# Six of seven convolution taps moved from VectorE to ScalarE and an adding DMA

## The chip, the cores and the metric

The kernel runs on one core of one Trainium2 chip. The core has five engines with a program each: TensorE (PE in the profile), VectorE (DVE), ScalarE (ACT), GpSimd (POOL) and SyncE (SP, which only issues DMAs here). Sixteen DMA engines carry all transfers. The metric is the device time of one launch in microseconds; lower is better.

## The reference

Two blocks follow one another. First a causal depthwise convolution with 7 taps over the sequence; the weights are soft-maxed over the taps and shared by the 24 channels of a head. Then a dense layer with silu and a second dense layer.

```python
w = np.exp(weight - weight.max(-1, keepdims=True)); w = w / (w.sum(-1, keepdims=True) + 1e-09)  # (8, 7)
x_pad = np.concatenate([zeros(B, 6, D), x], axis=1)      # x: (8, 4096, 192)
out = np.einsum('hk,bskhg->bshg', w, windows(x_pad))     # 7 taps, 8 heads of 24 channels
h = out.reshape(32768, 192) @ moe_w_in                   # (192, 2048)
return (h * (1 / (1 + np.exp(-h)))) @ moe_w_out          # (2048, 192)
```

(The lines are shortened; `windows` stands for the gather of seven shifted rows.) Everything is float32.

## The kernel before

The 32768 tokens are worked off in 32 blocks of 1024 (NB). A block holds two halves of 512 tokens: channels lie on partitions, 64 channels of the first half on partitions 0 to 63 and the same 64 of the second half on 64 to 127; the 192 channels make three channel groups k = 0, 1, 2. So one tile of 128x512 is one channel group of a block.

A block goes through these stages:

- *Load and turn* (`load`, L181; `turn_in`, L465). SP loads the block's tokens into the tile `nat` (two of them, used in turn). VectorE turns each channel group into `xt`, of which there is one only; its six first columns are the halo, filled by `halo_in` with a small copy on Pool (L486) or a memset (L480) and a DMA.
- *Convolution* (`conv`, L490 to L502). For channel group k and tap i the source is `xt` shifted by i columns, the target the same channel group of `nat`, which holds the sum. Tap 0 is a ScalarE activation with the tap's weights as scale (L496) and writes `nat`; taps 1 to 6 are a VectorE scalar_tensor_tensor (L499) each, `nat = xt * tap + nat`. That is 18 of them in a block.
- *Spread and windows* (`spread`, L516; `win`, L533 and L536). SP copies `nat` into `dups`, and VectorE forms sums and differences of the channel groups of the two halves, `win`.
- *Products* (`product`, L625, and `plain`, L642). The first dense layer is done by a scheme that saves multiplications: 5 groups (g) of 15 products (r), each summed in PSUM banks in three chains. ScalarE copies intermediate banks into tiles `u` (L674), VectorE combines them with other banks (L668), ScalarE takes the silu (L686, L691) into tiles `g`.
- *Down products* (`sum_g`, L709; `out_slot`, L741). VectorE forms differences of `g` tiles (`t`), and PE multiplies by the second layer's weights. ScalarE copies parts out of the accumulators (`yx`, `cmb`; L799, L804, L807), VectorE adds them (L819), turns them back (L829), and SP stores them (L838).

The tiles `u` are ten in number and are kept in a list, `free`: a step that needs one takes the first (`free.pop(0)`), and the step that has read it last appends it. The list is handled while the program is built, in the order in which the steps are written; the waits that it makes necessary are put in from the use of the tiles.

The order of all steps is written out by hand in the string `PLAN`: one block's stretch is some 130 slots, each with tokens that `step` (L858) turns into calls. A token is a name with digits; a prefix `-` means the block before, `=` two before, `+` the next. `P` is a product, `L` a plain one, `u`, `X`, `a`, `b`, `S` the copies, sums and silus on a product chain, `D` and `t` the down products of the block before, `sp` the spread, `w` the windows. `v.ki` is `conv(b + 1, k, i)`, so the convolution belongs to the next block. The tokens `v` stand in this order: 20 and 10 at the end of the stretch before; 00, 21, 22, 11, 12, 23, 13, 01, 14, 24, 02, 03, 25, 15, 26 among the down products; 16, 04, 05, 06 among the first products. `START` is the same for the first blocks. `pin` keeps an instruction in its written place on its engine; what isn't pinned (the halo copy on Pool, for one) may be moved by the scheduler. DMAs that SP issues form a queue in order; so do those that Pool issues.

The main loop runs over b from 3; with the `v` tokens meaning block b + 1, the main loop convolves blocks 4 to 31, and `START` the earlier ones.

Of the kernel before, what the change touches and what calls it, by code (L numbers as in the profile page):

```python
# [11 lines left out]
AF = mybir.ActivationFunctionType  # L12
ALU = mybir.AluOpType
# [4 lines left out]
def kernel(  # L18
# [24 lines left out]
    nc = tc.nc  # L43
# [111 lines left out]
    def pin(ins):  # L155
        return tc.keep_in_program_order(ins)
# [61 lines left out]
    for k in range(NK):  # L218
        rows_k = hot[SQ * k : SQ * k + SQ]
        for sign, base in ((1, 0), (-1, grp - 1)):  # L220
            pool.affine_select(
                out=rows_k,
                in_=rows_k,
# [7 lines left out]
    for e in range(2):  # L231
        half = one_hot[R * e : R * e + R].rearrange("p (a c) -> p a c", a=2)
        pool.affine_select(
            out=half,
            in_=half,
# [254 lines left out]
    def conv(b, k, i):  # L490

        src = xts[b][:, k, i : i + TB]
        dst = nats[b][:, k, :, :].rearrange("p k c -> p (k c)")
        tap = taps[:, k, i : i + 1]
        if i == 0:
            pin(nc.scalar.activation(dst, src, AF.Copy, scale=tap))  # L496
        else:
            pin(
                nc.vector.scalar_tensor_tensor(  # L499
                    out=dst, in0=src, scalar=tap, in1=dst, op0=ALU.mult, op1=ALU.add  # L500
                )
            )  # L502
# [153 lines left out]
    us, free = {}, []  # L656
# [201 lines left out]
    def step(b, token):  # L858
# [19 lines left out]
        elif name[0] in "uXabS":  # L878
            sums_h(b, name, *digits)
        elif name == "t":  # L880
            sum_g(b, *digits)
        elif name[0] == "D":
            i, (j, e) = int(name[1]), digits
            for half in range(2) if i == 3 and b == NB - 1 else (None,):
                out_slot(b, j, i, e, half)
        elif name[0] in "Mzyx":
            merge(b, name, *digits)
        elif name == "o":
            turn_out(b, *digits)
        elif name == "st":  # L890
            store_out(b, *digits)
        elif name == "dp":
            next(downs)
        elif name == "cp":
            copy_plain(b, *digits)
        elif name == "go":
            pool.tensor_copy(warm, nats[1][:, digits[0], 0, 0:1])
            for g in (2, 3):
                for e in range(2):
                    combine(g, e)  # L900
        elif name == "ld":
            if b + 1 < NB:
                load(b + 1, digits)
        elif b + 1 < NB:
            {"i": turn_in, "ha": halo_in, "v": conv, "sp": spread, "w": win}[name](
                b + 1, *digits[: 1 + (name == "v")]
            )
# [122 lines left out]
    for j in (1, 2):  # L1030
        load_in(j, nc.sync)
    turn_in(0, 2)
    conv(0, 2, 0)
    for n in range(2):
        act.copy(dups[0][:, n, 0, :], by_pe[0][n])
    for i in range(1, K):
        conv(0, 2, i)
    src = nats[0][:, 2, :, :].rearrange("p k c -> p (k c)")
# [72 lines left out]
```

## Time and profile before

| | |
|---|---|
| median of 3 runs | 2348.94 us (2348.9 to 2348.98) |
| span of the profiled execution, first to last instruction | 2347.5 us |
| median of the runs less that span | 1.4 us |
| granted TensorE clock | 1.000 |
| chain that ended last | PE 99% |
| DMA traffic | 106.56 MB, mean 45 GB/s |
| Pool's software queue (q0) | 448 packets, 1.58 MB |

The page of a profile shows one execution. The profiled execution has no time of its own in the list of runs; its span and the difference above stand for it. For each engine the page gives the busy time, its share of the span and the number of instructions. A row of a group has line, engine and operation, what is written and read, then the count, the busy time and the mean of one in ns, then the idle time of that engine just before these instructions and what ended most of it. A timeline row has start and length in us, then the operation, and in brackets the idle time before it with what ended it. A DMA row has the issuing queue, the count, the size and the median time from issue to landing. PEld is the load of weights into TensorE, which runs beside the matmuls.

### The profile page before, as it was taken

What the parts mean: (1) busy time and instruction counts of PE and PEld (TensorE: products, weight loads), DVE (VectorE), ACT (ScalarE), POOL (GpSimd) and SP (SyncE); (2) the same over time, 40 slices, a digit from 0 to 9 for tenths busy, and PEclk for the clock granted to TensorE, in tenths of its full rate; (3) what the DMA queues carried; (4) which work ended last, traced back from release to release, by engine and by line L of the source; (5) the groups of instructions that cost most, each with busy time, mean ns of one, the idle gap of its engine ahead of it and who ended that gap; (6) DMA issues with size and microseconds to landing.
All of it is one profiled execution on the core that took longest, in us unless ns stands there. A gap on an engine that the chain in (4) does not pass through costs nothing.

```text
span 2347.5 us, 43988 instructions
## 1 busy us (share of the span) xinstructions
PE 2340.3 (100%) x17630; PEld 1061.0 (45%) x17630; DVE 2099.6 (89%) x2877; ACT 1187.3 (51%) x2275; POOL 96.8 (4%) x168
## 2 busy tenths in 40 slices
PE   9999999999999999999999999999999999999998
PEld 4344444444444444434444444444444444444445
DVE  8899989899899998998998999989999989899876
ACT  4345644456544466444564445654446644456443
POOL 4920000000000000000000000000000000000000
PEclk9999999999999999999999999999999999999999
DMA  7232212222121221222221222212222212222111
GB/s 158 52 66 48 47 27 47 38 53 53 29 41 36 53 53 31 39 43 46 53 49 31 42 38 53 53 29 42 36 53 53 38 33 45 43 53 44 20 24 25
DMA packets 451245, 106.56 MB, mean 45 GB/s; under 512 B 423584, under 2 KB 428704, under 8 KB 451040
## 3 DMA queue, kind: packets, MB, share of 16 engines
q1 hardware_dynamic: 447392, 101.78, 23.7%
q8 instruction: 138, 2.26, 0.4%
q0 software_dynamic: 448, 1.58, 0.3%
q10 hardware_dynamic: 3200, 0.39, 0.1%
q14 instruction: 67, 0.55, 0.1%
HBM read 31.46 MB, written 25.17 MB: 24 GB/s over the span
## 4 chain that ended last, share of the span: by engine, by line
PE 99%; DVE 0%; ACT 0%; issue 0%; ACTq 0%
PE ps L741 47%; PE ps L625 42%; PE ps L642 5%; PE ps L762 2%; PE ps L571 2%; PE ps L1010 1%; PE ps L423 0%; DVE t L709 0%; ACT g L686 0%; DVE cmb L163 0%; ACT u L163 0%; DVE osb L163 0%; DVE osb L829 0%; DVE g L668 0%; PE ps L449 0%
## 5 line engine op out<-in xcount | busy, mean ns | idle before, releaser
L625 PE MATMUL ps<-win,wr 64*128 64x512 f32 x1550 | 720.3, 597 | 0.0
L741 PE MATMUL ps<-g,wo 128*32 128x512 f32 x2976 | 702.4, 593 | 0.0
L625 PE MATMUL ps<-win,ws 64*128 64x512 f32 x1550 | 631.3, 595 | 0.0
L741 PE MATMUL ps<-t,wo 128*32 128x512 f32 (+2 forms) x4528 | 545.7, 446 | 0.0
L674 ACT COPY u<-ps 128x512 f32<-128x512 f32 x775 | 446.8, 586 | 173.6 <-PE ps L625 161.4
L741 PE MATMUL ps<-t,wx 128*32 128x512 f32 x2976 | 495.5, 592 | 0.1
L625 PE MATMUL ps<-dup,wr 64*128 64x512 f32 x868 | 425.4, 593 | 0.0
L499 DVE SCALAR_TENSOR_TENSOR nat<-xt,taps,nat 128x512 f32<-128x512 f32 x564 | 411.3, 753 | 3.8 <-ACT nat L496 3.6
L686 ACT ACTIVATE g<-g 128x512 f32<-128x512 f32 x465 | 286.1, 633 | 231.5 <-DVE g L668 231.5
L804 ACT COPY yx<-ps 32x512 f32<-32x512 f32 x150 | 86.9, 579 | 574.0 <-PE ps L741 572.3
L709 DVE TENSOR_TENSOR t<-g 128x1024 f32<-128x1024 f32 x248 | 300.6, 1219 | 51.1 <-PE ps L741 43.4
L625 PEld LDWEIGHTS ps<-win,wr 64*128 64x128 f32 x1550 | 275.6, 186 | 150.4 <-issue 67.8
L668 DVE TENSOR_TENSOR g<-u,ps 128x512 f32<-128x512 f32 x465 | 311.2, 680 | 28.8 <-PE ps L625 14.6
L625 PE MATMUL ps<-dup,ws 64*128 64x512 f32 x682 | 324.2, 599 | 0.0
L709 DVE TENSOR_TENSOR t<-g,t 128x1024 f32<-128x1024 f32 x248 | 301.8, 1217 | 12.2 <-PE ps L741 9.4
L741 PEld LDWEIGHTS ps<-t,wo 128*32 128x32 f32 x4528 | 186.7, 110 | 274.1 <-issue 247.6
L625 PEld LDWEIGHTS ps<-win,ws 64*128 64x128 f32 x1550 | 254.7, 186 | 110.5 <-issue 40.8
L686 ACT ACTIVATE g<-ps 128x512 f32<-128x512 f32 x465 | 266.8, 597 | 41.1 <-PE ps L625 38.4
L668 DVE TENSOR_TENSOR ps<-u,ps 128x512 f32<-128x512 f32 x310 | 214.7, 692 | 43.7 <-ACT g L686 19.0
L741 PE MATMUL ps<-g,wx 128*32 128x512 f32 x1488 | 250.5, 592 | 0.0
L741 PEld LDWEIGHTS ps<-g,wo 128*32 128x32 f32 x2976 | 170.2, 110 | 120.9 <-issue 118.9
L741 PEld LDWEIGHTS ps<-t,wx 128*32 128x32 f32 x2976 | 120.5, 110 | 217.5 <-issue 202.3
(90 smaller groups left out, 1764.5 us busy)
## 6 DMA issues: line engine op xcount, KB each, us to landing
dup<-nat SPq DMA_DIRECT2D x345, 128.0 KB, 2.3
nat<-in_x_dram SPq DMA_DIRECT2D x382, 64.0 KB, 2.4
out_dram<-osb SPq DMA_DIRECT2D x376, 64.0 KB, 2.0
raw<-in_moe_w_out_dram SPq DMA_DIRECT2D x8, 384.0 KB, 3.6
raw<-in_moe_w_in_dram SPq DMA_DIRECT2D x12, 192.0 KB, 4.7
ws<-wr POOLq DMA_DIRECT2D x8, 192.0 KB, 5.0
raw<-in_moe_w_in_dram SPq DMA_DIRECT2D x6, 128.0 KB, 3.1
xt<-xt SPq DMA_DIRECT2D x31, 4.5 KB, 1.9
```

Of the source, the lines that this page charges most:

```text
L499: nc.vector.scalar_tensor_tensor(out=dst, in0=src, scalar=tap, in1=dst, op0=ALU.mult, op1=ALU.add)
L571: nc.tensor.matmul(hs[a, n, e], rows(wr[j], e)[:, a, k, :], rows(d, e)[:, n, k, :], start=k == 0, stop=k == NK - 1,)
L625: nc.tensor.matmul(to[:, cols], raw(g, *LEFT[e][r], e), rhs[:, cols], start=first, stop=True, skip_group_check=True,)
L642: nc.tensor.matmul(banks[PLAIN_BANKS[n and 1 + e]][:, cols], rows(wr[j] if own == e else ws[j], e)[:, a, k, :], rows(dups[b], e)[:, SLOT[e ...
L668: pin(nc.vector.tensor_tensor(out_, u, v, op=op))
L674: pin(nc.scalar.copy(us[b, g, o][:, cols], t1[:, cols]))
L686: pin(nc.scalar.activation(h, src, AF.Silu))
L709: pin(nc.vector.tensor_tensor(t[i // 2][:, i % 2, :], u, v, op=ALU.subtract))
L741: nc.tensor.matmul(accs[b][at][SQ * q : SQ * q + SQ, to], lhs[:, e, SQ * k : SQ * k + SQ], rhs[:, e, ts(q, TB // 4) if i == 5 else to], st ...
L762: nc.tensor.matmul(banks[DOWN_BANKS[k]][R * n : R * n + R, :], wo[j][:, a, e, R * k : R * k + R], gs[b, j, a][:, n, e, :], start=j == 0 an ...
L804: pin(nc.scalar.copy(to, acc[3 * (name[0] == "x") + k][n:P, :]))
L1010: nc.tensor.matmul(by_pe[k][n], rows(diag, n)[:, k, i, :], rows(xts[0], n)[:, k, i : i + TB], start=i == 0, stop=i == K - 1,)
```

## The change

In `conv`, taps 1 to 6 (the second to the seventh) of blocks 4 to 31 take another form. A spare tile z is taken from the front of the list `free`; ScalarE multiplies the shifted source by the tap's weights into z; a DMA on Pool's queue adds z to the channel group of `nat`; and z is appended to the list at once. Blocks 0 to 3 and tap 0 stay as they are, and `PLAN` and `START` stay unchanged, so each tap keeps its place in the written order.

```diff
         if i == 0:
             pin(nc.scalar.activation(dst, src, AF.Copy, scale=tap))
+        elif b > 3:
+            z = free.pop(0)
+            pin(nc.scalar.activation(z, src, AF.Copy, scale=tap))
+            pin(nc.gpsimd.dma_start(out=dst, in_=z, accum_op=ALU.add))
+            free.append(z)
         else:
             pin(
                 nc.vector.scalar_tensor_tensor(
```

In the built program the adding DMAs stand on Pool's queue in the order of the tokens. Each waits for its ScalarE multiply and for the adding DMA before it on the same channel group. A ScalarE instruction that writes a tile z or u waits for the adding DMA that last read that tile. The halo copy on Pool stands between the DMAs of taps 05 and 06.

## The prediction

> **What bounds the kernel now.** I read the page first, then the timeline of single blocks, then the waits. The page says which engine has no idle time:
>
> ```profile
> span 2347.5 us, 43988 instructions
> PE 2340.3 (100%) x17630; PEld 1061.0 (45%) x17630; DVE 2099.6 (89%) x2877; ACT 1187.3 (51%) x2275; POOL 96.8 (4%) x168
> L499 DVE SCALAR_TENSOR_TENSOR nat<-xt,taps,nat 128x512 f32<-128x512 f32 x564 | 411.3, 753 | 3.8 <-ACT nat L496 3.6
> ```
>
> PE bounds it; the row to be replaced (L499) is VectorE work that lies beside PE. The wait list gives the length of a block, since the halo copy on Pool runs once in each: 1368.0/19 = 72.0 us.
>
> ```profile
> POOL xt L486 <- ACT u L674: 1368.0, 19, 72.4
> PEld ps L625 <- DVE ps L668: 57.8, 214, 0.8
> PEld ps L625 <- ACT u L674: 15.6, 61, 0.6
> ```
>
> How much of the 72.0 us is PE's own work? In the timeline two matmul halves start every 0.43 us (1264.41, 1264.84, 1265.27). Each matmul of the source leaves two records. A block has 75 products, so 75 x 0.428 = 32.1 us; the plain part is 12 full-width records, 6 pairs or 2.6 us; the down part has 320 full and 64 quarter-width records, four at a time, 34.3 + 1.7 us. Together 70.7 us. So at most 1.3 us a block is stall, and no relief of another engine can give more than 28 x 1.3 = 37 us. The two lower lines say that VectorE and ScalarE both end such short waits.
>
> Then one block, in windows (PE, PEld, DVE, ACT, POOL busy; clock; DMA share; GB/s):
>
> ```profile
> 1226.00:1235.00 9.00, 9.00 (x104) 3.02 (x100) 8.54 (x10) 2.27 (x4) 0.00 (x0) 1.00 0.66 134
> 1235.00:1259.00 24.00, 24.00 (x262) 8.19 (x256) 21.01 (x27) 3.28 (x8) 0.00 (x0) 1.00 0.04 6
> 1259.00:1276.00 17.00, 17.00 (x86) 8.97 (x84) 15.54 (x25) 12.88 (x26) 0.19 (x1) 1.00 0.27 50
> 1276.00:1295.00 19.00, 19.00 (x89) 11.54 (x90) 17.05 (x27) 16.34 (x31) 0.00 (x0) 1.00 0.26 43
> ```
>
> The reader is to see that in the down stage (to 1259) ScalarE and the DMA engines are nearly free, while in the product stage (from 1259) ScalarE is 76 to 86% busy and its copies of PSUM banks (L674) set when PE may write these banks again.
>
> **The change, part by part.** 18 taps in each of 28 blocks, 504 of the 564 rows of L499.
>
> *VectorE* loses 504 x 0.729 us (411.3/564) = 367 us, 13 us a block. Fourteen of the 18 lie in the down stage, where PE seldom waits for VectorE; four (1261, 1263, 1270, 1272 us) in the product stage. Gain on the path: between 0 and 1.3 us a block; I take 0.2, since only the four count, and the waits above are each short.
>
> *ScalarE* gets 504 multiplies. The nearest row is its first tap, L496, which the next instruction follows 0.62 us later (1217.15 to 1217.77): 312 us, busy 51 to 64%. In the down stage they fill an idle stretch of 17.8 us. In the product stage the taps 16, 04, 05 and 06 stand in front of bank copies and silus, each 0.6 us; the gaps there are 0.3 to 1.0 us, so each makes the next copy 0 to 0.6 us late, and PE after it. Between 0 and 2.4 us a block; I take 0.4.
>
> *Pool* gets 504 issues of 0.65 us (the Pool issues of L347 ran 523 to 878 ns), 328 us on an engine that is idle. But Pool is in order, and each adding DMA waits for the one before it on the same channel group, as it reads and writes the same tile. What is queued behind such a wait is every later tap, and once a block the halo copy (0.19 us), which has 13 us until SP needs it (its DMA is issued at 1284). Who waits for the DMA itself: the spread DMAs (sp.1 at 1272, sp.0 and sp.2 in the next block), and, because a spare tile goes back into the free list at once, ScalarE at its reuse. That is the new wait: bank copies of the product stage now get tiles whose DMA must have read them.
>
> *The chain.* Call L the time from one adding DMA's issue to that of the next that depends on it, I = 0.65 us the issue. Taps 21 and 22 go early (about 1226 and 1226 + L). The others are released when ScalarE has done the silu at 1233.93:
>
> ```profile
> 1227.21 0.63 ACT L686 ACTIVATE g<-g 128x512 f32<-128x512 f32 x1
> 1233.93 0.63 ACT L686 ACTIVATE g<-g 128x512 f32<-128x512 f32 x1 [6.09 <-DVE g L668]
> 1252.36 0.58 ACT L804 COPY yx<-ps 32x512 f32<-32x512 f32 x1 [17.80 <-PE ps L741]
> 1267.19 0.59 ACT L674 COPY u<-ps 128x512 f32<-128x512 f32 x1 [0.63 <-PE ps L625]
> 1270.66 0.58 ACT L674 COPY u<-ps 128x512 f32<-128x512 f32 x1 [1.05 <-PE ps L625]
> ```
>
> so tap 11 issues at T = 1235.2. In Pool's order 11, 12, 23, 13, 01, 14, 24, 02, 03, 25, 15, 26, 16, 04 the issues fall at T + 0, L, L+I, 2L, 2L+I, 3L, 3L+I, 3L+2I, 4L+2I, 4L+3I, 4L+4I, 5L+3I, 5L+4I, 5L+5I. The copies that reuse these tiles: the one at 1267.19 (T + 32.0) takes tap 26's, done at 6L+3I, so L may be 5.0; the one at 1263.28 (T + 28.1) takes tap 03's, done at 5L+2I, so 5.4. Tap 05 is multiplied in its place behind the copy at 1269.1 (issue T + 35.3), tap 06 follows one L later and ends at T + 35.3 + 2L; its tile is wanted by a copy at T + 42.3 (1205.43 one block earlier). That gives L = 3.5; but this bank is next written six products after its own, 2.6 us, of which 0.9 go to the matmul's end and the copy, so PE feels it from about L = 4.2. Above 4.2 a block loses 2 us for each us of L, above 5.0 six to eight, since that many links stand ahead.
>
> *L itself* is not in the trace: there is no adding DMA. The nearest rows:
>
> ```profile
> dup<-nat SPq DMA_DIRECT2D x345, 128.0 KB, 2.3
> ws<-wr POOLq DMA_DIRECT2D x8, 192.0 KB, 5.0
> xt<-xt SPq DMA_DIRECT2D x31, 4.5 KB, 1.9
> xt<-in_x_dram POOLq DMA_DIRECT2D x2, 1.5 KB, 3.1
> xt<-in_x_dram SPq DMA_DIRECT2D x1, 1.5 KB, 2.6
> ```
>
> Low end: 128 KB more than almost nothing cost 0.4 us, so 256 KB plain 1.9 + 0.8 = 2.7. High end: the Pool row scaled to 256 KB, 1.9 + 3.1 x 4/3 = 6.0; it ran in the start-up, with the DMA engines busy, and the down stage has a share of 0.04. Value: 1.9, twice 0.8 because the target is read too, 0.5 for Pool instead of SP (3.1 against 2.6), 0.2 for waking Pool: 4.2 to 4.3, nearest to the quiet SBUF-to-SBUF row. That is at the knee.
>
> A rule on this price: the Trainium skill's page "DMA: Bandwidth & Descriptors", section "Anatomy of one DMA", has 2.0 us and bytes/436e3 for a Pool DMA, which for 256 KB would make an estimate of 2.6 us and the chain cost nothing; it does not name adding ones, and no row here shows one. Its section "Rules for kernel authors" speaks against the change: an adding DMA must wait for the completion of an earlier one on the same bytes, which is the chain above.
>
> *Sum* a block: -0.2 (VectorE) + 0.4 (ScalarE's places) + 0.3 (L at 4.3, two links of 0.1 and some spill) = +0.5 us, times 28 = +14 us. The first four blocks, start and end are not touched. Against the profiled execution's span, 2347.5 + 14 = 2361.5; the median of the runs, 2348.94, lies 1.4 us above that span, so 2363.
>
> **The rivals.**
> 1. *The chain is too slow.* With L = 5.5, 32 us after T are no longer enough: 6L+3I = 35.0 against 32.0, then taps 05 and 06 behind; about 7 us a block, 196 us, 2545. With L = 6.0, 11 us a block, 2657. For it: the Pool row of 5.0 us. Against: that row's traffic.
> 2. *Other sign: VectorE's relief pays.* If L stays under 4.2 and the product stage's stalls are mainly VectorE's (57.8 us of waits against 15.6 for ScalarE), 0.3 to 1.2 us a block come back: 8 to 34 us, 2315 to 2341. It decides when the four ScalarE insertions cost less than the four VectorE removals. Against: ScalarE's own gaps there are just as short.
> 3. *Hidden on all sides.* PE is saturated, both effects cancel within 0.2% (4.7 us, about what a measurement of this kernel can tell from no change): 2344 to 2354.
>
> **How the numbers follow.** Forecast (0.2 to 2% slower, 2354 to 2396): 0.38. Rival 1 (above 2396): 0.32. Rival 2: 0.22. Rival 3: 0.08. So faster 0.22, same 0.08, slower 0.70. The likeliest one's own range is 2354 to 2396; 8 in 10 need part of rivals 1 and 2: from 2332 (about half of rival 2) to 2580 (L of about 5.6, beyond which I leave 0.1).
>
> **What the profile after would show.** L499's row at 60, ScalarE near 1500 us, POOL near 420 us, 504 new issues "nat<-u" of 256 KB on POOLq with a landing near 4 us: right. If they land above 5 us, ScalarE's copies and multiplies wait for DMA, PE shows idle in the product stage, and the halo period grows by the same amount: rival 1. If the period falls under 72.0: rival 2. The prediction is wrong above all if L is off by half a microsecond or more, or if the tiles' reuse distance is not what the order of the free list makes it.

## The result and the profile after

The changed kernel takes 2362.43 us (median of four runs, 2360.49 to 2365.5) against 2348.92 us before: a ratio of 1.0058, 95% interval 1.0044 to 1.0072. The forecast was 2363 and slower. The profiled execution is the fastest of the four (2360.49 us); its span is 2358.8 us, 11.3 us more than before, while the medians lie 13.5 us apart. These lines of its page answer to the lines shown of before:

```profile
span 2358.8 us, 45531 instructions
PE 2350.1 (100%) x17630; PEld 1053.1 (45%) x17630; DVE 1784.5 (76%) x2373; ACT 1488.6 (63%) x2779; POOL 531.0 (23%) x672
q0 software_dynamic: 73024, 133.73, 33.7%
L500 POOL DMA_DIRECT2D nat<-u x504 | 431.9, 957 | 1598.0 <-ACT u L499 643.4
nat<-u POOLq DMA_DIRECT2D x504, 256.0 KB, 4.0
dup<-nat SPq DMA_DIRECT2D x345, 128.0 KB, 3.0
```

VectorE lost 315 us of busy time, ScalarE got 301, Pool issues 504 DMAs. They land 4.0 us after their issue (median; 3.2 to 6.2). SP's spread DMAs now land in 3.0 us instead of 2.3. That is the adding DMAs' doing: in the runs below it is 2.3 us without them and 2.6 with half their bytes. The wait list shows the wait that the prediction named, ScalarE's bank copies at reused tiles, and a longer PE wait on a silu (8.5 us in 30 waits before):

```profile
ACT u L679 <- DMA nat<-u: 28.3, 24, 2.4
PEld ps L630 <- ACT u L679: 29.0, 88, 1.3
PEld ps L630 <- ACT g L691: 27.7, 59, 0.6
```

In one block's timeline of ScalarE it is the copy that was expected at T + 42.3, which reuses tap 06's tile:

```profile
1282.01 0.58 ACT L679 COPY u<-ps 128x512 f32<-128x512 f32 x1 [0.27 <-PE ps L630]
1283.46 1.79 ACT L679 COPY u<-ps 128x512 f32<-128x512 f32 x3 [0.87 <-DMA nat<-u]
```

Where the 11.3 us lie is seen best from block to block. The copy into `cmb` runs once in each block; the distance of its starts in ScalarE's timeline is the block's length. The usual block is the median of the 28 that carry the change:

| kernel | usual block, us | 28 x (usual - 72.14) | sum above the usual block | blocks over 0.15 us above it |
|---|---|---|---|---|
| before | 72.14 | 0 | 0.1 | 0 |
| changed | 72.37 | 6.4 | 5.1 | 9 |

6.4 + 5.1 = 11.5 us is the difference of the two spans. So there are two costs: 0.23 us in every block, and a second one in nine blocks only, up to 1.46 us in one. Not all nine are the DMAs' doing: two of them, the first and the 23rd (0.35 and 0.23 us), are as uneven in the run below that leaves the taps out (0.35 and 0.33). The second cost may also be why the four runs lie 5 us apart; only one of them has a profile, so this is not shown.

### The profile page after: what moved, and what is told of

Read it like the earlier page. It is cut to its first block, busy times and chain, and to the rows that moved or that the text cites. A ratio compares the mean times of both kernels' runs of the same rounds, so it can differ in the third digit from the quotient of the medians.

```text
span 2358.8 us, 45531 instructions
## 1 busy us (share of the span) xinstructions
PE 2350.1 (100%) x17630; PEld 1053.1 (45%) x17630; DVE 1784.5 (76%) x2373; ACT 1488.6 (63%) x2779; POOL 531.0 (23%) x672
## 4 chain that ended last, share of the span: by engine, by line
PE 98%; DVE 1%; DMA 0%; ACT 0%; SPq 0%; issue 0%; ACTq 0%
PE ps L746 47%; PE ps L630 42%; PE ps L647 5%; PE ps L767 2%; PE ps L576 2%; PE ps L1015 1%; DVE t L714 0%; DMA dup<-nat 0%; PE ps L423 0%; ACT g L691 0%; DMA nat<-u 0%; SPq L843 0%; DVE g L673 0%; DVE cmb L163 0%; ACT u L163 0%
## 5 line engine op out<-in xcount | busy, mean ns | idle before, releaser
L500 POOL DMA_DIRECT2D nat<-u x504 | 431.9, 957 | 1598.0 <-ACT u L499 643.4
L630 PE MATMUL ps<-win,ws 64*128 64x512 f32 x1550 | 638.3, 599 | 0.9 <-ACT u L679 0.9
L499 ACT ACTIVATE u<-xt,taps 128x512 f32<-128x512 f32 x504 | 340.0, 717 | 1.1
L824 DVE TENSOR_TENSOR cmb<-cmb,ps 96x512 f32<-96x512 f32 x150 | 102.2, 681 | 181.7 <-ACT yx L809 180.7
```

The source lines that it names most:

```text
L499: pin(nc.scalar.activation(z, src, AF.Copy, scale=tap))
L500: pin(nc.gpsimd.dma_start(out=dst, in_=z, accum_op=ALU.add))
L630: nc.tensor.matmul(to[:, cols], raw(g, *LEFT[e][r], e), rhs[:, cols], start=first, stop=True, skip_group_check=True,)
L824: pin(nc.vector.tensor_tensor(out_, u, v, op=ALU.add))
```

## The experiments

All were timed beside the kernel before, which took 2349.04 to 2349.07 us there.

**ScalarE and VectorE without the DMAs.**

```diff
             pin(nc.scalar.activation(z, src, AF.Copy, scale=tap))
-            pin(nc.gpsimd.dma_start(out=dst, in_=z, accum_op=ALU.add))
             free.append(z)
```

> Taps two to seven of blocks 4 to 31 are multiplied on ScalarE into the spare tile, but nothing adds the tile (the sum of these taps is left out). So ScalarE's insertions and VectorE's relief stay, the adding DMAs are gone. Theory (the terms of the prediction): -0.2 us for VectorE and +0.4 us for ScalarE's places remain, +0.3 us for the DMAs' links goes: about 2355, 2351 to 2358. Rival A (ScalarE's places cost all of it, the DMA waits are hidden): 2360 to 2364, as the changed kernel. Rival B (the DMAs cost all of it, and VectorE's relief outweighs ScalarE's places): below 2347.

Measured: 2356.91 us, ratio 1.0032 (1.0021 to 1.0044); the usual block 72.39. So 5.5 us of the change's 13.5 are the DMAs' by the medians (3.3 by the spans of the profiled executions), and they are not in the usual block.

**VectorE's relief alone** (the diff stands against the changed kernel).

```diff
         elif b > 3:
-            z = free.pop(0)
-            pin(nc.scalar.activation(z, src, AF.Copy, scale=tap))
-            pin(nc.gpsimd.dma_start(out=dst, in_=z, accum_op=ALU.add))
-            free.append(z)
+            return
```

> Taps two to seven of blocks 4 to 31 are left out altogether: VectorE's relief alone, nothing on ScalarE, no DMA. Theory: 0.2 us a block come back, 2343; bounds 2312 (all of the 1.3 us a block that PE stalls) to 2349 (nothing). If VectorE ends most of PE's stalls, as the wait list's 57.8 us against 15.6 us for ScalarE could be read: 2315 to 2330.

Measured: 2348.54 us, ratio 0.9997 (0.9988 to 1.0007), a usual block of 72.09 to 72.10 us. So no gain is clear of the noise: 0.5 us by the medians, 0.05 us by the usual block, and at most 2.8 us, 0.1 a block, by the interval. Theory's 0.2 was too much, and the hope of rival 2 is gone altogether. PE's waits on VectorE did not leave with the work; the row of before had 57.8 us in 214:

```profile
PEld ps L627 <- DVE ps L670: 47.4, 160, 0.7
PEld ps L627 <- ACT u L676: 15.3, 60, 0.6
```

So most of them belong to the product chains themselves (PE, copy, combine, PE) and not to the convolution's place between them, and the 10 us of waits that did go left the time as it was.

**ScalarE's insertions alone.**

```diff
         elif b > 3:
             z = free.pop(0)
             pin(nc.scalar.activation(z, src, AF.Copy, scale=tap))
-            pin(nc.gpsimd.dma_start(out=dst, in_=z, accum_op=ALU.add))
+            pin(
+                nc.vector.scalar_tensor_tensor(
+                    out=dst, in0=src, scalar=tap, in1=dst, op0=ALU.mult, op1=ALU.add
+                )
+            )
             free.append(z)
```

> The kernel before with the ScalarE multiplies into spare tiles added, which nobody reads; the sum stays on VectorE. So ScalarE's insertions alone. Theory: +0.4 us a block, 2360 (2354 to 2368). Rival A (ScalarE's places are the whole of the change's cost and VectorE's relief adds nothing): 2362 to 2366. Rival B (ScalarE's places are free, the DMA waits are the cost): 2348 to 2351.

Measured: 2356.43 us, ratio 1.003 (1.0019 to 1.0042), a usual block of 72.39 us. The diff stands against the changed kernel. ScalarE's insertions cost 7.4 us, neither nothing nor all. With the first two runs the parts nearly add: 7.4 (ScalarE) - 0.5 (relief) + 5.5 (DMAs) = 12.4 of 13.5. What is missing is the relief itself: beside the insertions it gives nothing (2356.91 us with it, 2356.43 without), and 7.8 for both together + 5.5 = 13.3 of 13.5.

**Eleven spare tiles** (`hot` is moved in the same way as `zeros`; run twice, the profile is the second one's).

```diff
-    upool = ctx.enter_context(tc.tile_pool(name="up", bufs=10))
+    upool = ctx.enter_context(tc.tile_pool(name="up", bufs=11))
-    zeros = const.tile([P, P], F32, name="zeros") 
+    zeros = upool.tile([P, TB], F32, tag="u", name="zeros")[:, 0:P]
-    free.extend(upool.tile(...) for _ in range(10))
+    free.extend(upool.tile(...) for _ in range(11))
```

> The changed kernel with eleven spare tiles in the list instead of ten (two constants used in the start-up move into this pool to make room; the result is complete). The copy that reuses tap 06's tile is now the next one on ScalarE, 0.86 us later, and tap 05's multiply no longer waits for tap 04's DMA. Theory: the wait of ScalarE's copies for the adding DMAs, 28.3 us in all in the changed kernel, falls to below 8 us, and the time to 2354 to 2359. Rival A (ScalarE's places): 2361 to 2364, with the waits gone all the same.

Measured: 2359.66 us, ratio 1.0043 (1.0027 to 1.006), just above the theory's 2354 to 2359.

> The run with eleven tiles again, for its profile: the first one's profiled execution was disturbed and can't be read. Theory now: usual blocks stay at 72.37, the uneven ones (eight above 72.5 in the changed kernel) become fewer or smaller, ScalarE's copies wait below 8 us for adding DMAs instead of 28.3: 2359 to 2360. Rival: the uneven blocks are as many, and the gain comes from an even shorter usual block.

Measured: 2359.32 us, ratio 1.0047 (1.0032 to 1.0062). The usual block stays at 72.38; six blocks instead of nine are uneven, with 3.5 us instead of 5.1. The waits at reused tiles:

```profile
ACT u L679 <- DMA nat<-u: 6.6, 9, 1.3
DVE t L714 <- DMA dup<-nat: 10.6, 3, 3.7
```

So tile reuse carries a part of the uneven blocks, as expected: about 3 us by the medians (of the changed kernel's runs, which spread over 5), 1.5 by the sum above the usual block. The second line is another kind, below.

**The four middle taps earlier.**

```diff
-    "... -D2.30 v.02 | ... -D5.30 v.03 | -D0.10 v.25 | -D3.21 -z1.0 v.15 ... -x2.1 v.26 ..."
+    "... -D2.30 v.02 v.03 v.25 v.15 v.26 | ... -D5.30 | -D0.10 | -D3.21 -z1.0 ... -x2.1 ..."
```

> The changed kernel with the tokens of taps 03, 25, 15 and 26 moved in the written list to stand right behind tap 02, so that ScalarE multiplies them in its idle stretch ahead of the copies of the accumulators (yx, cmb) instead of between them. The result is complete. Theory now: ScalarE's places cost 7.4 us (e3), and they cost it where PE's plain products wait for the late yx copies (23.5 us of waits in e3, none before), so most of it goes: 2354 to 2357, and a usual block falls from 72.37 to 72.15 us. Rival (as the prediction had it: the four places in the product stage, taps 16, 04, 05 and 06): 2361 to 2364, a block of 72.37.

Measured: 2364.02 us, ratio 1.0061 (1.0046 to 1.0076), a usual block of 72.38. My theory of that hour fell. The 23.5 us of PE waits on `yx` did vanish, but they had cost nothing: the kernel before has the same pause of 0.84 us at this place, put down to "issue". The totals agree: before has 69.4 us of "issue" in 218 at this line of the code, the run with ScalarE's insertions 45.9 in 190 and the 23.5 in 28. (The moved multiplies also wait 104.9 us for reused tiles, so the time of this run alone would not settle it; the pause does.) Here is its row of before, then that of the run with ScalarE's insertions alone, from PE's weight-load timelines:

```profile
1258.67 0.18 PEld L642 LDWEIGHTS ps<-dup,ws 64*128 64x128 f32 x1 [0.84 <-issue]
```

```profile
1262.46 0.18 PEld L651 LDWEIGHTS ps<-dup,ws 64*128 64x128 f32 x1 [0.84 <-ACT yx L808]
1278.68 0.29 PEld L634 LDWEIGHTS ps<-dup,wr 64*128 64x128 f32 x2 [0.59 <-ACT g L695]
```

The label changed, the pause did not. The row at 1278.68 has no fellow in the kernel before; it led to the next two runs.

**Only the last four places.** ScalarE multiplies, read by nobody, in the places of taps 16, 04, 05 and 06; VectorE keeps the sum.

```diff
+            if (k, i) in ((1, 6), (0, 4), (0, 5), (0, 6)):
+                z = free.pop(0)
+                pin(nc.scalar.activation(z, src, AF.Copy, scale=tap))
+                free.append(z)
```

> The kernel before with ScalarE multiplies into spare tiles, read by nobody, only in the places of taps 16, 04, 05 and 06, in the product stage (e3 had all 18). The sum stays on VectorE and the result is complete. Theory now: these four cost nothing or little, the others' places carry e3's 7.4 us: 2348.5 to 2351. Rival (the prediction's place): 2354 to 2356.5, as e3.

Measured: 2354.65 us, ratio 1.0024 (1.0014 to 1.0033), a usual block of 72.34. The prediction's place was right after all: these four carry 0.20 of the 0.25 us a block.

**The same without tap 06** (the list of places ends at `(0, 5)`).

> As the run with the last four places, but with ScalarE multiplies only in the places of taps 16, 04 and 05; tap 06's, which stands right ahead of a run of four silus, is gone. The sum stays on VectorE and the result is complete. Theory now: in that run PE waited 0.59 us once a block for the last of those silus, so tap 06's place alone costs the 0.20 us a block: 2348.5 to 2350. Rival (each of the four a quarter): 2352.5 to 2354.

Measured: 2351.42 us, ratio 1.0011 (1.0001 to 1.002), a usual block of 72.22. Between theory and rival: tap 06's place alone costs 0.12 us a block, the other three 0.08 together. PE's waits on these silus fall from 25.1 us in 58 to 8.5 in 30, as before. In ScalarE's timeline of the run with the last four, tap 06's multiply is the row at 1274.80, right ahead of the silus; the last of them frees the bank that PE waits for:

```profile
1274.80 0.73 ACT L500 ACTIVATE u<-xt,taps 128x512 f32<-128x512 f32 x1
1275.43 0.62 ACT L696 ACTIVATE g<-g 128x512 f32<-128x512 f32 x1
1275.95 1.56 ACT L696 ACTIVATE g<-ps 128x512 f32<-128x512 f32 x3
```

```profile
1277.56 0.29 PEld L635 LDWEIGHTS ps<-dup,wr 64*128 64x128 f32 x2 [0.59 <-ACT g L696]
```

**Tap 06 behind the silus, in the changed kernel.**

```diff
-    "... P8.0 u1.4 v.06 S5.0 | ... S3.0 a0.0 S2.4 | ... S3.4 | ... b1.4 S4.4 | ..."
+    "... P8.0 u1.4 S5.0 | ... S3.0 a0.0 S2.4 | ... S3.4 | ... b1.4 S4.4 v.06 | ..."
```

> The changed kernel with tap 06's token moved in the written list to stand behind the four silus instead of ahead of them (ten tiles, result complete). Theory now: a usual block falls from 72.37 to 72.15 or 72.20 us, 5 to 6 us in all; the uneven blocks may also get rarer, since the copy that reuses this tap's tile is two copies further: 2355 to 2358. Rival (the place is not the cause): 2361 to 2364.

Measured: 2358.12 us, ratio 1.0039 (1.0025 to 1.0054). The usual block falls to 72.27, by 0.10 us, nearly tap 06's 0.12; 72.15 to 72.20 had been expected, and the time lies at the upper edge of its range. Nine blocks stay uneven, with 5.5 us.

**Half the columns.**

```diff
-            pin(nc.gpsimd.dma_start(out=dst, in_=z, accum_op=ALU.add))
+            pin(nc.gpsimd.dma_start(out=dst[:, 0 : TB // 2], in_=z[:, 0 : TB // 2], accum_op=ALU.add))
```

> The changed kernel whose adding DMAs add only the first 256 of 512 columns (the other half of the sum of taps two to seven is left out): 128 KB each, all else the same. Theory now: the DMAs' 5.5 us (2362.4 less e1's 2356.9) come from a few blocks in which they and SP's transfers hold each other up; with half the bytes the landing falls from 4.0 to about 3.4 us, the uneven blocks go, and the time is e1's: 2356.5 to 2359. Rival (a steady cost of each DMA, Pool's issue or the semaphores): 2361 to 2363, with even blocks.

Measured: 2356.94 us, ratio 1.0033 (1.002 to 1.0046): the time of the run without any DMA (2356.91). The landing is 3.0 us, and the sum above the usual block is 0.8 us, as without DMAs (0.7). So neither the 504 issues nor their semaphores cost anything here; the longer transfer of the full columns does.

**Longer links.**

```diff
             pin(nc.gpsimd.dma_start(out=dst, in_=z, accum_op=ALU.add))
+            pin(nc.gpsimd.dma_start(out=dst[:, 0:64], in_=z[:, 0:64], accum_op=ALU.add))
```

> The changed kernel with a second small adding DMA (64 columns, 32 KB) behind each of the 504, on the same bytes, so that each link of the chain is longer by one small DMA (those columns are then added twice, and the result is not the reference's). L goes from about 4.3 to 6.5 to 7 us and the issue from 0.85 to 1.7 us. Theory, by the prediction's chain (6L+3I and what follows it against the 32 us to the copy): 16 to 24 us a block, 450 to 670 us in all: 2810 to 3030. Rival (the chain has slack that the recurrence does not see, as the reuse order or PE's slack is larger): below 2600.

Measured: 3640.82 us, ratio 1.5488 (1.5463 to 1.5514), blocks of 113.7 to 122 us: 46 us a block instead of 16 to 24. My expectation missed what an in-order queue does. Pool's timeline of this run shows it (L500 the tap's DMA, L501 the small one):

```profile
1803.34 0.84 POOL L500 DMA_DIRECT2D nat<-u  x1 [1.86 <-DMA nat<-u]
1806.89 0.86 POOL L501 DMA_DIRECT2D nat<-u  x1 [2.71 <-DMA nat<-u]
1807.43 1.19 POOL L500 DMA_DIRECT2D nat<-u  x1
1811.32 0.86 POOL L501 DMA_DIRECT2D nat<-u  x1 [2.70 <-DMA nat<-u]
1811.85 1.19 POOL L500 DMA_DIRECT2D nat<-u  x1
```

The small DMA stands in the queue waiting for the large one just issued, so no other channel group's large DMA can be in flight meanwhile. A pair takes 4.1 to 4.4 us here, so 18 of them nearly 80 us, in a block that had 72. Between one block's last pair and the next block's first another 25 us pass (1843.30 to 1868.18 in the same timeline). In the changed kernel the interleaving of three channel groups hides a part of L; here it is gone. ScalarE's copies then wait 910 us in all for these DMAs. The granted TensorE clock was 0.842 in this run against 1.000 before; how much of the 46 us the lower clock adds was not separated.

**Eleven tiles and tap 06 later together.**

> Eleven tiles and tap 06's token behind the four silus, together (result complete): the best form of the change that these runs point to. Theory: the two gains add, 2362.4 - 2.8 - 5.5 = 2354, 2352 to 2357; still above the kernel before, since VectorE's relief gives nothing (0.4 us in the run of the relief alone) and tap places and traffic are left. Rival (the gains are the same one): 2357 to 2360.

Measured: 2357.13 us (2355.47 to 2357.93), ratio 1.0033 (1.002 to 1.0046). The usual block is 72.27 and ScalarE's copies wait 2.2 us in all, but six blocks stay uneven with 5.2 us. The gains add only in part: 3.1 and 4.3 us alone, 5.3 together, at the border of what theory and rival had expected. It is the fastest complete form of the change here, and still 8 us above the kernel before. The run of the relief says why none can be much better than before: leaving the taps out altogether gains 0.5 us.

**What is left of the uneven blocks.** In the chain of waits of the changed kernel's profile one such block reads like this, first the chain, then VectorE's timeline:

```profile
1375.46 1.60 SPq L843
1377.70 3.75 DMA dup<-nat
1381.47 1.24 DVE t L714
```

```profile
1376.69 1.21 DVE L714 TENSOR_TENSOR t<-g 128x1024 f32<-128x1024 f32 x1
1381.47 1.23 DVE L714 TENSOR_TENSOR t<-g 128x1024 f32<-128x1024 f32 x1 [3.57 <-DMA dup<-nat]
```

VectorE stands still for 3.57 us ahead of the sum `t`, and PE then idles 0.5 us. The sum takes a buffer in which the stores' `osb` stood, so by the code it is the three stores that it must wait for; the profile names a spread DMA, which SP issued right behind them. SP's three stores took 2.5 us to issue instead of the usual 1.41. SP's queue did that before as well, in the same block, and there the same sum waited 0.64 us, put down to a store, and the block kept its 72.14 us:

```profile
1224.49 1.41 SPq L838 DMA_DIRECT2D out_dram<-osb  x3
1368.79 2.42 SPq L838 DMA_DIRECT2D out_dram<-osb  x3
```

```profile
1372.90 1.23 DVE L709 TENSOR_TENSOR t<-g 128x1024 f32<-128x1024 f32 x1 [0.64 <-DMA out_dram<-osb]
```

So the likeliest reading is that a late store meets the first adding DMA and seven spread DMAs (DMA share 0.96 to 0.98 there), and lands later still: the slowest of the three landed after 4.1 us, before after 3.0. Which of the two kinds of DMA ends VectorE's wait was not separated by a run.

With eleven tiles such chains stand at 1157, 1375 and 1810 us, three or six blocks apart. The rhythm is older than the change: in the kernel before, from 936 to 2018 us, every third block (every 216.4 us) has three stores that take 1.9 to 2.9 us to issue. The DMA queue that the profile calls "instruction" (q8) has a packet in the same 3 to 4 us in all eight groups of three stores that took over 1.8 us there, and in two of the 47 others. So SP's delay goes along with a packet of that queue; that the packet is the cause was not tested. Four of the nine uneven blocks of the changed kernel (3.6 of the 5.1 us), and the four that remain with eleven tiles beside the first and the 23rd, are such third blocks.

## Why the prediction was right, and where its terms were not

The time (2363 against 2362.4), the sign and the chain of causes held, but all three terms of the sum were too large. In us for the 28 blocks: VectorE -5.6, measured -0.5; ScalarE's places +11.2, measured +7.4; the DMAs +8.4, measured +5.5. The errors nearly cancel, so that the time was met within 1 us is luck; the sign and the two costs are not.

- *PE bounds the kernel.* Right: 1.4 us a block is all that is not PE's own work, and the relief of another engine was bounded by it. (The prediction's 72.0 us is the halo copy's wait; with the copy's own 0.19 it is the block's 72.14.)
- *VectorE's relief, -0.2 us a block.* Mis-sized: about -0.02 by the time, -0.05 by the usual block. The step that failed is the reading of the wait list, that "only the four count, and the waits above are each short" leaves something to gain; 47.4 of the 57.8 us stay without the taps. VectorE's busy time fell by 315 us, not 367.
- *ScalarE's places, +0.4 us.* Right in kind and place, mis-sized: 0.25 us a block, of which tap 06 has 0.12, the taps 16, 04 and 05 together 0.08, and the other fourteen 0.05. ScalarE's total rose to 1489 us, against 1500 forecast.
- *The issue, 0.65 us.* 0.854 us (median), so POOL is busy 531 us instead of some 420; it did not matter, as the run with half the columns shows.
- *L, 4.2 to 4.3 us.* In the run with longer links 3.55 us from issue to dependent issue (1803.34 to 1806.89 above), with no other large adding DMA in flight; in one block of the changed kernel 4.35 between taps 05 and 06 (1275.76 to 1280.11 in Pool's timeline) and 5.86 between taps 21 and 22, beside SP's transfers. So the value lay between two cases, and the knee at 4.2 was met in some blocks only. Its part of 0.2 us for waking Pool rests on no row; in the changed kernel an issue follows the end of its multiply by 0.29 us (1230.97 to 1231.26).
- *The issue times.* For taps 03 and 04 it was not the links that set them, as the prediction's list has it: in the same timeline Pool waits for ScalarE's multiply, which stands behind other ScalarE work (4.16 us for tap 03, 0.43 for tap 04). The reuse was read rightly all the same: all 24 waits of copies for adding DMAs are at the one copy that the prediction named for tap 06's tile.
- *The DMAs' term, +0.3 us a block ("two links of 0.1 and some spill").* The sum was nearly right (8.4 against 5.5 us), its shape was not: the usual block pays nothing, although its copy waits 0.9 us, as the prediction's slack allows; seven blocks pay 0.2 to 1.5 us (the nine less the two that are uneven without DMAs). The prediction had left out that SP's transfers are themselves made later by the adding DMAs.
- *Rival 1 (chain too slow)* did not come. That PE pays many times over when the chain no longer fits was confirmed by the longer links, but its size there was set by the in-order queue, and perhaps by the lower clock, and not by the formula.
- *Rival 2 (relief pays)* is excluded by the run of the relief alone.

On the price of an adding DMA: the rule of the Trainium skill's page "DMA: Bandwidth & Descriptors", section "Anatomy of one DMA", makes an estimate of 2.6 us for 256 KB. Measured were 4.0 us for 256 KB (3.6 in the run with longer links), 3.0 for 128 KB and 2.2 for 32 KB. 4.0, 3.0 and 2.2 lie on 2.0 us plus 1.0 us for each 128 KB. The least landings, 3.2, 2.6 and 2.1 us, rise by only 0.6 us from 128 to 256 KB. So the fixed part agrees with the page's 2.0 us, and the rate of 436 GB/s, 0.3 us for 128 KB, was not reached. How much of that is the adding and how much the traffic beside it is open, since no plain DMA of this size ran on Pool's queue here after the start-up.

## What to carry to other kernels

When one engine has no idle time, price the relief of another by the run that leaves the work out, or by the bound of the stalls, and not by the wait list: here the list had 57.8 us of waits on VectorE, and leaving out 315 us of its work gave 0.5. An instruction added to an engine with gaps costs what it delays, so its place counts more than its length: one of eighteen multiplies, ahead of four silus, made up half of that cost. Where dependent DMAs share one queue, independent chains should alternate in it, and the transfers of other queues that the traffic makes late belong in the sum.

## What was not expected of the hardware

In this kernel's traffic an adding DMA from SBUF to SBUF took 2.0 us plus 1.0 us per 128 KB (median landings of 2.2, 3.0 and 4.0 us for 32, 128 and 256 KB, in three runs). Moving 132 MB in this way, with the DMA engines' queue share from 24 to 57%, left the usual block's length unchanged (72.37 us with, 72.39 without); its cost showed in a few blocks, most of it where SP's stores were slow to issue before the change too.
